# Last 64 GELU columns and the gate computed with tokens on partitions, in a gated mix of a state-space layer and a GELU feed-forward layer

## The chip, the cores and the metric

The kernel runs on one core of a Trainium2 chip. The metric is the time of one execution on the device, in microseconds (us). Beside it each run has a *span*, from the first to the last instruction of the profile. For the kernel before, the time is always 1.7 to 1.9 us longer than the span; this difference matters later.

Engines: PE is the tensor engine's matmul side, PEld its weight loads, DVE the vector engine, ACT the scalar (activation) engine, POOL the general-purpose one, SP the engine that issues most DMAs. "Moving columns" are the columns that a matmul streams through the array; the other operand, the weights, is loaded before. A *bank* is the piece of accumulation memory that a matmul writes.

## The reference, cut to what matters

There are 2,048 tokens of 640 values. A sigmoid gate per token mixes a state-space layer (`a`) with a feed-forward layer (`b`), whose hidden width is 1,728.

```
x = A_x                                             # [1, 2048, 640]
g = sigmoid((x * gate_w).sum(-1, keepdims=True))    # one number per token
a = state_space(x)                                  # input product, scan over tokens, output product, + x * Dskip
h = gelu(x @ w1 + b1)                               # [2048, 1728]
b = h @ w2 + b2
out = g * a + (1 - g) * b
```

1,728 is 13 x 128 + 64. The 14th tile of hidden columns has only 64 of them, and the kernel puts the gate's product beside it as a 65th column. This tile is what the change is about.

## The kernel before

Tokens go through in 4 chunks of 512. The first layer ("ff1") keeps the hidden columns on partitions: the weights of the matmul are a piece of `w1`, and the 512 tokens of the chunk move. The last tile thus streams all 512 columns for only 65 output partitions:

```
sizes = [P] * (KF - 1) + [F_LAST + 1]            # 13 tiles of 128, one of 65

def ff1_mm(p, c, kf, kd, t0=0, t1=CH):
    m = sizes[kf]
    w = ...                                       # m columns of w1, for the last tile 64 and gate_w
    nc.tensor.matmul(p[:m, t0:t1], lhsT=w, rhs=xT[c][:, kd, t0:t1], start=(kd == 0), stop=(kd == KD - 1))

def ff1_act(p, c, kf):
    m = min(sizes[kf], F - kf * P)
    nc.scalar.activation(out=gel[c][:m, kf, :], in_=p[:m, :], func=ACT.Gelu_apprx_tanh, bias=b1_c[:m, kf:kf + 1])
    if kf == KF - 1:
        # the gate: one partition, 512 tokens, then four DMAs that put it on the token partitions
        nc.scalar.activation(out=zrow[F_LAST:F_LAST + 1, :], in_=p[F_LAST:F_LAST + 1, :], func=ACT.Tanh, scale=0.5)
        for a in range(TPC):
            ti = c * TPC + a
            nc.sync.dma_start(out=gz[:, ti:ti + 1], in_=zrow[F_LAST:F_LAST + 1, a * P:(a + 1) * P])
```

The start loads its weights in pieces on the SP queue; `w1b` holds the hidden columns from 768 on:

```
for kd in range(KD):
    nc.sync.dma_start(out=w1b[kd][:, 0:F - cut1], in_=B_w1[kd * P:(kd + 1) * P, cut1:F])
# ... small parameters on the ACT queue, among them two loads of b1: 13 rows of 128, one row of 64 ...
nc.sync.dma_start_transpose(out=BT_re[:], in_=A_B_re[:, :])
nc.sync.dma_start_transpose(out=BT_im[:], in_=A_B_im[:, :])
```

The order on PE is: ff1 of chunk 0, then the state-space input product ("ssm") of chunk 0, ff1 and ssm of chunk 1, then for each chunk the second layer (`fin_b`) and the state-space output product (`fin_a`), with ssm and ff1 of the later chunks between.

Of the kernel before, what the change touches and what calls it, by code (L numbers as in the profile page):

```python
# [11 lines left out]
ACT = mybir.ActivationFunctionType  # L12
BF16 = mybir.dt.bfloat16
F32 = mybir.dt.float32
I32 = mybir.dt.int32

P = 128
T = 2048
D = 640
F = 1728  # L20
CH = 512
NCH = T // CH
KD = D // P
KS = D // P
KF = (F + P - 1) // P
F_LAST = F - (KF - 1) * P
NT = T // P
TPC = CH // P
HD = D // 2
FA = 6  # L30
# [8 lines left out]
def kernel(  # L39
# [19 lines left out]
    nc = tc.nc  # L59
# [4 lines left out]
    const = ctx.enter_context(tc.tile_pool(name="const", bufs=1))  # L64
# [7 lines left out]
    def bank(dtype=F32):  # L72
        return ps.tile([P, CH * 4 // (4 if dtype == F32 else 2)], dtype, name="bank")
# [3 lines left out]
    n1b = F - cut1 + 1  # L77
    xT = [const.tile([P, KD, CH], BF16, name=f"xT{c}") for c in range(NCH)]
    w1a = [const.tile([P, cut1], BF16, name=f"w1a_{kd}") for kd in range(KD)]
    w1b = [const.tile([P, n1b], BF16, name=f"w1b_{kd}") for kd in range(KD)]  # L80
# [6 lines left out]
    TSIN = const.tile([P, KS, CH], BF16, name="TSIN")  # L87
    ident = const.tile([P, P], BF16, name="ident")
    prmA = const.tile([3 * KS, P], BF16, name="prmA")
    NB = KS + KF  # L90
    prmB = const.tile([NB, P], BF16, name="prmB")
    colA = const.tile([P, 3 * KS], F32, name="colA")
    colB = const.tile([P, NB], F32, name="colB")
    Dbc = const.tile([P, D], BF16, name="Dbc")
    glast = const.tile([P, 2, KS], F32, name="glast")
    carry = const.tile([P, 2, KS], F32, name="carry")
    zrow = const.tile([P, CH], F32, name="zrow")
    gz = const.tile([P, NT], F32, name="gz")
    gcol = const.tile([P, 2, NT], F32, name="gcol")
    warm = work.tile([P, CH], BF16, name="v")  # L100
# [5 lines left out]
    lre_c = colA[:, 2 * KS:3 * KS]  # L106
    b1_c = colB[:, KS:NB]

# [15 lines left out]
    nc.sync.dma_start_transpose(out=xT[0][:, :, H * P:CH], in_=x2d[H * P:CH, :])  # L124
    for kd in range(KD):
        nc.sync.dma_start(out=w1b[kd][:, 0:F - cut1], in_=B_w1[kd * P:(kd + 1) * P, cut1:F])
    nc.gpsimd.memset(prmB[:], 0.0)
    make_identity(nc, ident[:])
    HC = CH // 4
    tfi = work.tile([P, HC], I32, name="e")  # L130
    nc.gpsimd.iota(tfi[:], pattern=[[1, HC]], base=0, channel_multiplier=0)
    nc.scalar.dma_start(out=prmB[KS:NB - 1, :], in_=B_b1[0:(KF - 1) * P].rearrange("(j p) -> j p", p=P))
    nc.scalar.dma_start(out=prmB[NB - 1:NB, 0:F_LAST], in_=B_b1[(KF - 1) * P:F].rearrange("(j p) -> j p", p=F_LAST))
    nc.scalar.dma_start(out=prmB[0:KS, :], in_=gate_w.rearrange("(j p) -> j p", p=P))
    nc.sync.dma_start_transpose(out=BT_re[:], in_=A_B_re[:, :])
    nc.sync.dma_start_transpose(out=BT_im[:], in_=A_B_im[:, :])
    nc.sync.dma_start_transpose(out=xT[1][:], in_=x2d[CH:2 * CH, :])
# [14 lines left out]
    class Clock:  # L152
        pe = 5.0
        act = 13.0
        dve = 0.0

    ck = Clock()
# [5 lines left out]
    def let_out(until):  # L163
        while pend:
            ready, cost, fn = pend[0]
            start = max(ck.dve, ready)
            if start >= until:
                return
            pend.pop(0)
            fn()  # L170
            ck.dve = start + cost
# [6 lines left out]
    def pe(cols):  # L178
        ck.pe += cols / 2400.0 + 0.002

    def act(cost):
        ck.act = max(ck.act, ck.pe + 0.2) + cost
        return ck.act
# [75 lines left out]
    hs = [None] * NCH  # L259
    gel = [None] * NCH  # L260
    gbs = [None] * NT
    sizes = [P] * (KF - 1) + [F_LAST + 1]

    def ff1_mm(p, c, kf, kd, t0=0, t1=CH):
        m = sizes[kf]
        w = w1a[kd][:, kf * P:kf * P + m] if kf < FA else w1b[kd][:, (kf - FA) * P:(kf - FA) * P + m]
        nc.tensor.matmul(p[:m, t0:t1], lhsT=w, rhs=xT[c][:, kd, t0:t1], start=(kd == 0), stop=(kd == KD - 1))  # L267
        pe(t1 - t0)

    def ff1_act(p, c, kf):  # L270
        m = min(sizes[kf], F - kf * P)
        nc.scalar.activation(out=gel[c][:m, kf, :], in_=p[:m, :], func=ACT.Gelu_apprx_tanh, bias=b1_c[:m, kf:kf + 1])  # L272
        act(0.69)
        if kf == KF - 1:
            nc.scalar.activation(out=zrow[F_LAST:F_LAST + 1, :], in_=p[F_LAST:F_LAST + 1, :], func=ACT.Tanh, scale=0.5)
            act(0.6)
            for a in range(TPC):
                ti = c * TPC + a
                nc.sync.dma_start(out=gz[:, ti:ti + 1], in_=zrow[F_LAST:F_LAST + 1, a * P:(a + 1) * P])

    def ff1(c, k0=0):
        for kf in range(k0, KF):
            p = bank()
            for kd in range(KD):
                ff1_mm(p, c, kf, kd)
            ff1_act(p, c, kf)
            let_out(ck.pe)

    def gel_tile(c):
        gel[c] = gelp.tile([P, KF, CH], BF16, name="gel")  # L290
        nc.gpsimd.memset(gel[c][F_LAST:F_LAST + 1, KF - 1, :], 1.0)


    gel_tile(0)
    banks = [bank() for _ in range(FA)]
    for kd in range(KD):
        for kf in range(FA):
            ff1_mm(banks[kf], 0, kf, kd, 0, HT)
# [10 lines left out]
    for kd in range(KD):  # L309
        for kf in range(FA):  # L310
            ff1_mm(banks[kf], 0, kf, kd, HT, CH)
        if kd == 2:
            nc.tensor.transpose(pA[:, P:P + NB], prmB[:], ident[0:NB, 0:NB])  # L313
            nc.vector.tensor_copy(out=colB[:], in_=pA[:, P:P + NB])
            for j in range(KD):
                nc.vector.tensor_copy(out=w1b[j][:, n1b - 1:n1b], in_=pA[:, P + j:P + j + 1])
    for kf in range(FA):
        ff1_act(banks[kf], 0, kf)
    ff1(0, FA)

    lo, hi = slice(0, HC), slice(HC, HB)
# [8 lines left out]
    for ks in range(KS):  # L330
        nc.vector.tensor_copy(out=TCOS[:, ks, 0:HB], in_=FC[:, ks, :])
        nc.vector.tensor_copy(out=TSIN[:, ks, 0:HB], in_=FS[:, ks, :])
        for dst, X, xs, Y in ((TCOS, FS, nsH, FC), (TSIN, FC, sH, FS)):
            t = work.tile([P, HB], F32, name="g")
# [194 lines left out]

    ssm(0)  # L530
    gel_tile(1)
    ff1(1)
    gates(0)
    ssm(1)
# [5 lines left out]
    load_xn(2)  # L540
    ssm(2)
    gel_tile(2)
    ff1(2)
    fin_b(1)
    gates(2)
# [41 lines left out]
```

## Time and profile before

The time before was 219.42 us, the median of 3 runs (219.11 to 219.45).

| what | value | view |
|---|---|---|
| span of the profiled run | 217.0 us | page, first line |
| PE busy | 212.2 us, 98% | page, part 1 |
| chain that ended last | 94% PE | page, part 4 |
| ff1 of a later chunk (14 tiles) | 15.11 us | windows |
| the last tile's 5 matmuls | 1.08 us | timeline |

First, lines of the page of the kernel before: span and number of instructions; busy time and share of each engine, with the number of its instructions; the DMA queue that fetches program code (packets, MB, share); and the chain of waits by engine.

```profile
span 217.0 us, 3363 instructions
...
PE 212.2 (98%) x1297; PEld 127.8 (59%) x1308; DVE 189.3 (87%) x393; ACT 94.1 (43%) x153; POOL 3.2 (1%) x12
...
q8 instruction: 10, 0.16, 0.3%
...
PE 94%; DMA 3%; issue 0%; SPq 0%; DVE 0%
```

PE sets the pace, with nothing but the first loads ahead of it. DVE waits once for the gate's DMA (`gz<-zrow`), for 1.9 us. The timeline of PE in the kernel before, around the last tile of chunk 0. Columns: start, duration, engine, line, what is written and read, weights (rows * columns), moving (rows x columns), count.

```profile
19.82 0.38 PE L267 MATMUL bank<-xT_76,w1b_85 128*65 128x512 bf16 x1
20.04 0.38 PE L267 MATMUL bank<-xT_76,w1b_86 128*65 128x512 bf16 x1
...
20.68 0.38 PE L267 MATMUL bank<-xT_76,w1b_89 128*65 128x512 bf16 x1
20.90 1.24 PE L448 MATMUL bank<-xT_76,BT_re 128*128 128x512 bf16 x5
```

Durations of matmuls overlap, so the *starts* are what counts: 216 ns apart, whether the weights have 65 columns or 128. And at the end of the same timeline, products of 128 columns:

```profile
213.32 0.44 PE L514 MATMUL bank<-CT_re,hs 128*128 128x128 bf16 x5
213.60 0.44 PE L514 MATMUL bank<-CT_im,hs 128*128 128x128 bf16 x5
```

Ten such matmuls, each with a full weight load of its own, start 56 ns apart (0.28 us for five). So weight loads hide at that pace. The Trainium skill ("TensorE: Matmul & The Clock Gate", section "Wait — 56ns, not 53.3ns?") gives moving columns / 2.4 GHz plus about 2.5 ns; these 56 and 216 ns agree.

The ff1 stretches of chunks 1, 2 and 3, in windows: from:to, length, then busy time and instructions of PE, PEld, DVE, ACT and POOL, the granted clock, DMA share, GB/s.

```profile
31.69:46.80 15.11, 15.01 (x69) 6.93 (x70) 14.63 (x40) 9.53 (x14) 0.00 (x0) 1.00 1.08 281
94.50:109.61 15.11, 15.01 (x70) 6.93 (x71) 14.81 (x27) 9.54 (x14) 0.00 (x0) 1.00 0.00 1
146.51:161.62 15.11, 15.01 (x69) 6.93 (x70) 14.83 (x28) 9.54 (x14) 0.00 (x0) 1.00 0.00 0
```

Two of its waits (who waited for what: us in total, times, longest), which the argument needs later:

```profile
DVE gcol L463 <- DMA gz<-zrow: 1.9, 1, 1.9
...
PEld L267 <- DMA w1b_89<-in_B_w_dram: 0.2, 1, 0.2
```

The second is small and easy to pass over. It says that in chunk 0 PE reaches `w1b` just as its last load lands: there is no slack there.

### The profile page before, as it was taken

What the parts mean: (1) busy time and instruction counts of PE and PEld (TensorE: products, weight loads), DVE (VectorE), ACT (ScalarE), POOL (GpSimd) and SP (SyncE); (2) the same over time, 40 slices, a digit from 0 to 9 for tenths busy, and PEclk for the clock granted to TensorE, in tenths of its full rate; (3) what the DMA queues carried; (4) which work ended last, traced back from release to release, by engine and by line L of the source; (5) the groups of instructions that cost most, each with busy time, mean ns of one, the idle gap of its engine ahead of it and who ended that gap; (6) DMA issues with size and microseconds to landing.
All of it is one profiled execution on the core that took longest, in us unless ns stands there. A gap on an engine that the chain in (4) does not pass through costs nothing.

```text
span 217.0 us, 3363 instructions
## 1 busy us (share of the span) xinstructions
PE 212.2 (98%) x1297; PEld 127.8 (59%) x1308; DVE 189.3 (87%) x393; ACT 94.1 (43%) x153; POOL 3.2 (1%) x12
## 2 busy tenths in 40 slices
PE   7999999999999999999999999999999999999994
PEld 4854444444577775444467777444457777777773
DVE  2899999969999999999999999999999999941153
ACT  2798656657696102556652200456663220022100
POOL 2001000000000000000000000000000000000000
PEclk9999999999999999999999999999999999999999
DMA  6999999970000025000000005100000000100011
GB/s 179 267 258 209 216 253 333 204 206 2 0 3 0 0 53 181 12 0 0 3 0 0 0 3 181 60 5 0 0 0 0 3 0 30 63 32 0 3 62 60
DMA packets 32326, 15.64 MB, mean 72 GB/s; under 512 B 25077, under 2 KB 32310, under 8 KB 32310
## 3 DMA queue, kind: packets, MB, share of 16 engines
q1 hardware_dynamic: 32098, 15.38, 28.2%
q8 instruction: 10, 0.16, 0.3%
q10 hardware_dynamic: 212, 0.04, 0.1%
q14 instruction: 6, 0.05, 0.1%
HBM read 7.22 MB, written 2.62 MB: 45 GB/s over the span
## 4 chain that ended last, share of the span: by engine, by line
PE 94%; DMA 3%; issue 0%; SPq 0%; DVE 0%
PE bank L495 28%; PE bank L267 26%; PE bank L514 20%; PE bank L448 20%; DMA xT_76<-in_A_x_dram 2%; DMA w1a_80<-in_B_w_dram 1%; SPq L116 0%; SPq L123 0%; DVE ot L519 0%; PE bank L313 0%
## 5 line engine op out<-in xcount | busy, mean ns | idle before, releaser
L495 PE MATMUL bank<-w_sb,gel 128*128 128x320 bf16 x448 | 61.6, 299 | 0.0
L495 PEld LDWEIGHTS <-gel 128*128 128x128 bf16 x448 | 43.7, 98 | 17.7
L272 ACT ACTIVATE gel<-bank,colB 128x512 bf16<-128x512 f32 (+1 forms) x56 | 37.3, 693 | 17.5 <-PE bank L267 17.5
L451 ACT ACTIVATE bu<-bank 128x512 bf16<-128x512 f32 x40 | 23.7, 597 | 38.9 <-PE bank L448 38.4
L514 PEld LDWEIGHTS <-hs 128*128 128x128 bf16 x330 | 31.8, 98 | 11.9
L404 DVE TENSOR_TENSOR_SCAN g<-r_c,carry,v 128x512 bf16<-128x512 f32 x30 | 37.1, 1270 | 0.0
L498 ACT ACTIVATE gb<-bank,gcol 128x320 f32<-128x320 f32 x32 | 16.4, 528 | 46.1 <-PE bank L495 44.6
L514 PE MATMUL bank<-CT_im,hs 128*128 128x320 bf16 (+2 forms) x165 | 27.1, 295 | 0.0
L514 PE MATMUL bank<-CT_re,hs 128*128 128x320 bf16 (+2 forms) x165 | 27.1, 295 | 0.0
L519 DVE SCALAR_TENSOR_TENSOR ot<-bank,gcol,gb 128x320 bf16<-128x320 f32 (+2 forms) x33 | 17.3, 532 | 8.6 <-PE bank L514 8.4
L481 DVE TENSOR_TENSOR bank<-xn,Dbc 128x320 f32<-128x320 bf16 (+2 forms) x33 | 14.5, 482 | 6.9 <-ACT gb L498 6.9
L448 PEld LDWEIGHTS <-BT_im 128*128 128x128 bf16 x100 | 9.8, 98 | 11.8
L448 PEld LDWEIGHTS <-BT_re 128*128 128x128 bf16 x100 | 9.8, 98 | 11.5
L385 DVE TENSOR_TENSOR v<-wa,wb 128x512 bf16<-128x512 bf16 x40 | 15.2, 421 | 0.6
L385 DVE TENSOR_TENSOR wa<-TCOS,g 128x1024 bf16<-128x1024 bf16 x20 | 13.7, 685 | 0.1
L385 DVE TENSOR_TENSOR wb<-TSIN,g 128x1024 bf16<-128x1024 bf16 x20 | 13.7, 684 | 0.0
L385 DVE TENSOR_TENSOR wb<-TSIN,bu 128x1024 bf16<-128x1024 bf16 x20 | 13.7, 684 | 0.0
L385 DVE TENSOR_TENSOR wa<-TCOS,bu 128x1024 bf16<-128x1024 bf16 x20 | 13.7, 683 | 0.0
L404 DVE TENSOR_TENSOR_SCAN g<-r_c,v 128x512 bf16<-128x512 f32 x10 | 11.8, 1210 | 0.0
L385 DVE TENSOR_TENSOR hs<-wa,wb 128x512 bf16<-128x512 bf16 x20 | 8.5, 424 | 0.7
L385 DVE TENSOR_TENSOR hs<-wb,wa 128x512 bf16<-128x512 bf16 x20 | 8.4, 418 | 0.0
L448 PE MATMUL bank<-xT_76,BT_im 128*128 128x512 bf16 x25 | 6.2, 379 | 0.0
(153 smaller groups left out, 243.1 us busy)
## 6 DMA issues: line engine op xcount, KB each, us to landing
out_dram<-ot SPq DMA_DIRECT2D x15, 160.0 KB, 1.8
w_sb<-in_B_w_dram SPq DMA_DIRECT2D x1, 2080.0 KB
xn<-in_A_x_dram SPq DMA_DIRECT2D x3, 640.0 KB, 4.8
xn<-in_A_x_dram SPq DMA_DIRECT2D x2, 320.0 KB
gz<-zrow SPq DMA_DIRECT2D x16, 0.5 KB, 2.0
w1b_85<-in_B_w_dram SPq DMA_DIRECT2D x1, 240.0 KB
w1b_86<-in_B_w_dram SPq DMA_DIRECT2D x1, 240.0 KB, 3.7
w1b_87<-in_B_w_dram SPq DMA_DIRECT2D x1, 240.0 KB
```

Source lines behind the costliest of these rows:

```text
L267: nc.tensor.matmul(p[:m, t0:t1], lhsT=w, rhs=xT[c][:, kd, t0:t1], start=(kd == 0), stop=(kd == KD - 1))
L272: nc.scalar.activation(out=gel[c][:m, kf, :], in_=p[:m, :], func=ACT.Gelu_apprx_tanh, bias=b1_c[:m, kf:kf + 1])
L385: nc.vector.tensor_tensor(out=o, in0=a, in1=b, op=op)
L404: nc.vector.tensor_tensor_scan(s["g"][:, ri, :], r_c[:, ks:ks + 1].to_broadcast([P, CH]), s["v"][:, ri, :], init, ALU.mult, ALU.add)
L448: nc.tensor.matmul(p[:], lhsT=BT[:, kd, ks * P:(ks + 1) * P], rhs=xT[c][:, kd, :], start=(kd == 0), stop=(kd == KD - 1))
L451: nc.scalar.activation(out=bu[:, ri, :], in_=p[:], func=ACT.Identity)
L481: dve_now(ck.pe, 0.45, lambda: nc.vector.tensor_tensor(out=p[:, 0:d1 - d0], in0=xn[c][:, a, d0:d1], in1=Dbc[:, d0:d1], op=ALU.mult))
L495: nc.tensor.matmul(p[:, 0:d1 - d0], lhsT=gel[c][:m, kf, lo:lo + P], rhs=w2_sb[:m, kf, d0:d1], start=(kf == 0), stop=(kf == KF - 1))
L498: nc.scalar.activation(out=gb[:, d0:d1], in_=p[:, 0:d1 - d0], func=ACT.Identity, scale=gcol[:, 1, ti:ti + 1])
L514: nc.tensor.matmul(p[:, 0:d1 - d0], lhsT=hs[c][:, j, lo:lo + P], rhs=CT[:, j % KS, d0:d1], start=False, stop=(j == 2 * KS - 1), skip_group ...
L519: nc.vector.scalar_tensor_tensor(out=ot[:, d0:d1], in0=p[:, 0:d1 - d0], scalar=gcol[:, 0, ti:ti + 1], in1=gbs[ti][:, d0:d1], op0=ALU.mult, ...
```

## The change

The intent: for the last tile let the 65 columns of `w1` move, and make the tokens the weights. A chunk then takes 4 token tiles x 5 input tiles = 20 matmuls of 65 moving columns, 1,300 columns in the place of 2,560. The gate comes out with tokens on partitions, where it is wanted, so its DMAs go. The bias now runs along the free dimension, while the activation call used so far takes one bias for each partition (`b1_c[:m, kf:kf + 1]`); so it is put into the bank first (the bank is "seeded"), by PE in chunk 0 and by ACT in the others. A DMA transpose turns the 64 GELU columns back for the second layer.

```
-    nc.scalar.dma_start(out=prmB[NB - 1:NB, 0:F_LAST], in_=B_b1[(KF - 1) * P:F]...)        # one row of b1
+    nc.sync.dma_start(out=b1x[:, 0:F_LAST], in_=B_b1[F - F_LAST:F]....to_broadcast([P, F_LAST]))   # after w1b, before BT_re
...
+    def last_bank(c):
+        p = bank()
+        pv = p[:, 0:TPC * NL].rearrange("p (a n) -> p a n", a=TPC)
+        if c == 0:
+            for a in range(TPC):
+                nc.tensor.matmul(pv[:, a, :], lhsT=ident[:], rhs=b1x[:], start=(a == 0), stop=True, skip_group_check=True)
+            return p, pv
+        nc.scalar.activation(out=pv, in_=b1x[:]....to_broadcast([P, TPC, NL]), func=ACT.Identity)
+        return p, pv
+
+    def last_tile(c, p, pv):
+        for a in range(TPC):
+            for kd in range(KD):
+                nc.tensor.matmul(p[:, a * NL:(a + 1) * NL], lhsT=xT[c][:, kd, a * P:(a + 1) * P],
+                                 rhs=w1b[kd][:, n1b - NL:n1b], start=False, stop=(kd == KD - 1), skip_group_check=True)
+        nc.scalar.activation(out=gelN[c % 2][:, :, 0:F_LAST], in_=pv[:, :, 0:F_LAST], func=ACT.Gelu_apprx_tanh)
+        nc.scalar.activation(out=gz[:, c * TPC:(c + 1) * TPC], in_=..., func=ACT.Tanh, scale=0.5)
+        nc.sync.dma_start_transpose(out=gel[c][:, KF - 1, :]..., in_=gelN[c % 2][:]...)

     def ff1(c, k0=0):
-        for kf in range(k0, KF):
+        for kf in range(k0, KF - 1):
             p = bank()
+            if kf == KF - 3:
+                last = last_bank(c)
             ...
+        last_tile(c, *last)
```

More of the change, by code (lines that the diff above doesn't have):

```diff
@@ L89 @@
     prmA = const.tile([3 * KS, P], BF16, name="prmA")
-    NB = KS + KF
+    NB = KS + KF - 1
     prmB = const.tile([NB, P], BF16, name="prmB")
@@ L96 @@
     carry = const.tile([P, 2, KS], F32, name="carry")
-    zrow = const.tile([P, CH], F32, name="zrow")
+    b1x = const.tile([P, F_LAST + 1], BF16, name="b1x")
+    gelN = [const.tile([P, TPC, P], BF16, name=f"gelN{i}") for i in range(2)]
     gz = const.tile([P, NT], F32, name="gz")
@@ L126 @@
         nc.sync.dma_start(out=w1b[kd][:, 0:F - cut1], in_=B_w1[kd * P:(kd + 1) * P, cut1:F])
-    nc.gpsimd.memset(prmB[:], 0.0)
     make_identity(nc, ident[:])
@@ L131 @@
     nc.gpsimd.iota(tfi[:], pattern=[[1, HC]], base=0, channel_multiplier=0)
-    nc.scalar.dma_start(out=prmB[KS:NB - 1, :], in_=B_b1[0:(KF - 1) * P].rearrange("(j p) -> j p", p=P))
-    nc.scalar.dma_start(out=prmB[NB - 1:NB, 0:F_LAST], in_=B_b1[(KF - 1) * P:F].rearrange("(j p) -> j p", p=F_LAST))
+    nc.gpsimd.memset(b1x[:, F_LAST:F_LAST + 1], 0.0)
+    for i in range(2):
+        nc.gpsimd.memset(gelN[i][:, :, F_LAST:P], 0.0)
+        nc.gpsimd.memset(gelN[i][:, :, F_LAST:F_LAST + 1], 1.0)
+    nc.scalar.dma_start(out=prmB[KS:NB, :], in_=B_b1[0:(KF - 1) * P].rearrange("(j p) -> j p", p=P))
     nc.scalar.dma_start(out=prmB[0:KS, :], in_=gate_w.rearrange("(j p) -> j p", p=P))
+    nc.sync.dma_start(out=b1x[:, 0:F_LAST], in_=B_b1[F - F_LAST:F].rearrange("(o d) -> o d", o=1).to_broadcast([P, F_LAST]))
     nc.sync.dma_start_transpose(out=BT_re[:], in_=A_B_re[:, :])
@@ L261 @@
     gbs = [None] * NT
-    sizes = [P] * (KF - 1) + [F_LAST + 1]
     def ff1_mm(p, c, kf, kd, t0=0, t1=CH):
-        m = sizes[kf]
-        w = w1a[kd][:, kf * P:kf * P + m] if kf < FA else w1b[kd][:, (kf - FA) * P:(kf - FA) * P + m]
-        nc.tensor.matmul(p[:m, t0:t1], lhsT=w, rhs=xT[c][:, kd, t0:t1], start=(kd == 0), stop=(kd == KD - 1))
+        w = w1a[kd][:, kf * P:(kf + 1) * P] if kf < FA else w1b[kd][:, (kf - FA) * P:(kf - FA + 1) * P]
+        nc.tensor.matmul(p[:, t0:t1], lhsT=w, rhs=xT[c][:, kd, t0:t1], start=(kd == 0), stop=(kd == KD - 1))
@@ L268, in ff1_mm @@
         pe(t1 - t0)
     def ff1_act(p, c, kf):
-        m = min(sizes[kf], F - kf * P)
-        nc.scalar.activation(out=gel[c][:m, kf, :], in_=p[:m, :], func=ACT.Gelu_apprx_tanh, bias=b1_c[:m, kf:kf + 1])
+        nc.scalar.activation(out=gel[c][:, kf, :], in_=p[:, :], func=ACT.Gelu_apprx_tanh, bias=b1_c[:, kf:kf + 1])
         act(0.69)
-        if kf == KF - 1:
-            nc.scalar.activation(out=zrow[F_LAST:F_LAST + 1, :], in_=p[F_LAST:F_LAST + 1, :], func=ACT.Tanh, scale=0.5)
-            act(0.6)
-            for a in range(TPC):
-                ti = c * TPC + a
-                nc.sync.dma_start(out=gz[:, ti:ti + 1], in_=zrow[F_LAST:F_LAST + 1, a * P:(a + 1) * P])
+    NL = F_LAST + 1
@@ new lines, in last_bank @@
+    def last_bank(c):
+        p = bank()
+        pv = p[:, 0:TPC * NL].rearrange("p (a n) -> p a n", a=TPC)
+        if c == 0:
+            for a in range(TPC):
+                nc.tensor.matmul(pv[:, a, :], lhsT=ident[:], rhs=b1x[:], start=(a == 0), stop=True, skip_group_check=True)
+            return p, pv
+        nc.scalar.activation(out=pv, in_=b1x[:].rearrange("p (o n) -> p o n", o=1).to_broadcast([P, TPC, NL]), func=ACT.Identity)
+        act(0.4)
+        return p, pv
[4 more added lines that the diff above has]
+                                 rhs=w1b[kd][:, n1b - NL:n1b], start=False, stop=(kd == KD - 1), skip_group_check=True)
+                pe(76)
+        nc.scalar.activation(out=gelN[c % 2][:, :, 0:F_LAST], in_=pv[:, :, 0:F_LAST], func=ACT.Gelu_apprx_tanh)
+        act(0.45)
+        nc.scalar.activation(out=gz[:, c * TPC:(c + 1) * TPC], in_=pv[:, :, F_LAST:NL].rearrange("p a o -> p (a o)"), func=ACT.Tanh, scale=0.5)
+        act(0.2)
+        nc.sync.dma_start_transpose(out=gel[c][:, KF - 1, :].rearrange("p (a t) -> p a t", a=TPC),
+                                    in_=gelN[c % 2][:].rearrange("p a n -> p (a n)"))
@@ L287, in ff1 @@
             let_out(ck.pe)
+        last_tile(c, *last)
+        let_out(ck.pe)
     def gel_tile(c):
         gel[c] = gelp.tile([P, KF, CH], BF16, name="gel")
-        nc.gpsimd.memset(gel[c][F_LAST:F_LAST + 1, KF - 1, :], 1.0)
     gel_tile(0)
```

## The prediction

> **What bounds the kernel now.** The tensor engine alone. The page gives it 212.2 us of a 217.0 us span (98%), clock granted 0.999. A busy PE is no proof by itself, but the chain of waits agrees: 94% of it is matmuls and nearly all the rest (3%) is the first DMAs. No wait of PE on another engine is longer than 1.2 us, and that one is the start. In the timeline matmuls start at even steps that follow the moving columns: 215.8 ns for 512, 136 ns for 320, 82 ns for 192, 55.9 ns for 128, which is columns / 2.4 GHz plus about 2.5 ns. The Trainium skill ("TensorE: Matmul & The Clock Gate", Wait — 56ns, not 53.3ns?) states this formula, and the trace agrees. So time is moving columns.
>
> **What the change removes.** The 14th GELU tile holds only 64 columns and the gate, so 5 matmuls of 512 moving columns per chunk fill 65 of 128 output partitions: 5 x 215.8 = 1,079 ns on PE per chunk, 4.3 us in all. Also one ACT tanh on one partition (590 ns) per chunk, 16 small gate DMAs (2.0 us to landing each), and one DVE wait of 1.9 us for them (at about 47 us).
>
> **What it adds.** 20 matmuls of 65 moving columns per chunk, each with its own 128x128 weight load; in chunk 0 four more for the bias; in chunks 1 to 3 one ACT seeding of 128x260, estimated 0.45 us from 0.53 us for 128x320. One DMA transpose per chunk, and a bias broadcast DMA at the start. The 65-row contraction in the second matmul stays.
>
> **The cost that decides.** By the formula a 65-column matmul is 65/2.4 + 2.5 = 29.6 ns. The question is whether the weight load hides. In the trace it does at 55.9 ns per pair (128 columns), and once two weight loads stand 15 ns apart (after the 15- to 19-column transposes, L313). Loads of 128 columns take 98 ns, of 65 columns 112 ns, so a full load occupies the array for less than its latency. The same page (Back-to-back issue gap) gives 81 ns for a pair at 128 columns; this trace shows 55.9, so I do not use it. I estimate 32 ns per pair: 20 x 32 = 640 ns against 1,079, 0.44 us saved per chunk, 1.76 us in four; less 4 x 32 = 0.13 us for the seeds of chunk 0: **1.6 us**. If pairs cannot go below 55.9 ns, the chunk costs 1,118 ns and the change loses 0.4 us.
>
> **Critical path.** All PE time counts. The rest should hide: ACT has about 0.36 us idle per GELU tile, and the seed is needed two tiles (2.2 us) after it can start. The transposed tile is first read 10.8 us after the first-layer matmuls of its chunk at the least (chunk 0: at about 59.5 us, issue at about 43.6). DVE is full until 190 us, but loses its 1.9 us wait, about what PE gains. The nearest hazard is BT_im, landing near 20.6 us, read at 21.8: the broadcast ahead of it costs about 0.5 us and PE comes 0.3 us earlier, which leaves about 0.4 us.
>
> **Predicted: 217.8 us, 217.2 to 218.8 in 8 of 10.** Faster by over 2%: 0.01; within 2%: 0.97; slower: 0.02.
>
> **What would show it.** Right: starts of the 65-column matmuls 30 to 35 ns apart in the timeline; PE still without waits; first-layer stretch of chunks 1 to 3 shorter by about 0.44 us; the DVE wait on the gate DMA gone. Wrong: starts at 50 ns or more; PE waiting at BT_im, at the seed, or at the transposed tile; DVE lateness turning into PE waits for banks.

## The result, and the profile after

The changed kernel took 218.87 us, the median of 6 runs (218.09 to 219.39), against 219.38 us (219.11 to 219.64) for the kernel before. The ratio is 0.9974, with a 95% interval of 0.9954 to 0.9993: 0.6 us faster by the means where 1.6 were predicted, and just outside the range given. (Ratios here are the mean time of one kernel's fast runs over that of the other's of the same rounds, so not quite the ratio of the medians quoted. For after_row and before_pad_j4 the recorded ratio fits the means only without the slow profiled run; with it they would be 0.9983 and 1.0012.) In a second measurement, after_copy below, the same kernel had a ratio of 0.9946.

The page of the changed kernel:

```profile
span 216.4 us, 3467 instructions
...
PE 210.8 (97%) x1361; PEld 128.0 (59%) x1372; DVE 189.3 (87%) x393; ACT 91.8 (42%) x156; POOL 1.6 (1%) x12
...
PE 92%; DMA 4%; SPq 2%; issue 0%; DVE 0%
```

The timeline of PE around the last tile of chunk 0:

```profile
20.57 0.59 PE L268 MATMUL bank<-xT,w1b 128*128 128x512 bf16 x2
21.00 0.78 PE L293 MATMUL bank<-w1b,xT 128*128 128x65 bf16 x20
21.62 1.24 PE L473 MATMUL bank<-xT,BT_re 128*128 128x512 bf16 x4
```

Twenty matmuls take 0.62 us; read one by one they start 30.7 ns apart on average. That is the mechanism of the prediction, even a little better (32 ns was the estimate). The ff1 windows of chunks 1 to 3 confirm it:

```profile
32.41:47.05 14.64, 14.54 (x85) 6.94 (x85) 14.23 (x41) 9.54 (x15) 0.00 (x0) 1.00 1.08 263
94.75:109.39 14.64, 14.54 (x85) 6.98 (x86) 14.39 (x25) 9.54 (x15) 0.00 (x0) 1.00 0.00 1
146.29:160.93 14.64, 14.54 (x84) 6.98 (x85) 14.36 (x28) 9.54 (x15) 0.00 (x0) 1.00 0.00 0
```

15.11 has become 14.64: 0.47 us in each chunk. Nothing waits for the transposes, and the DVE wait on the gate DMA is gone. So the saving is there. Cut into three at two marks, the first ssm matmul and the first matmul of the last `fin_a`, the two profiles show where it went (starts read from the trace, us):

| stretch | before | after | difference |
|---|---|---|---|
| start to the first ssm matmul (holds ff1 of chunk 0) | 20.90 | 21.62 | +0.72 |
| from there to the first matmul of the last `fin_a` | 182.08 | 180.68 | -1.40 |
| from there to the end of the span | 13.99 | 14.10 | +0.11 |

The middle gained 3 x 0.47. The start, which should have become 0.34 us shorter (0.47 less 0.12 for the four bias matmuls), became 0.72 longer. The waits of PE in the changed kernel say on what:

```profile
PEld L268 <- DMA w1b<-in_B_w_dram: 1.2, 2, 0.6
...
PE bank L268 <- DMA xT<-in_A_x_dram: 0.4, 1, 0.4
...
PE bank L268 <- DMA w1b<-in_B_w_dram: 0.3, 1, 0.3
```

Read matmul by matmul, the changed kernel lost 0.57 us at 9.1 us, where PE waited for the second half of `xT`, and 0.73 us at 13.5 and 14.2 us before `w1b` matmuls; the kernel before lost 0.23 us at 8.8 us and nothing later. The broadcast was issued only at 9.1 us, so the first of these stops is not its doing.

And there was a second oddity. The time exceeds the span by 1.79 to 2.99 us in the six runs, where the kernel before has 1.7 to 1.9. Something outside the first and last instruction had become longer too.

### The profile page after: what moved, and what is told of

It is laid out like the page before. It is cut to its first block, busy times and chain, and to the rows that moved or that the text cites. A ratio compares the mean times of both kernels' runs of the same rounds, so it can differ in the third digit from the quotient of the medians.

```text
span 216.4 us, 3467 instructions
## 1 busy us (share of the span) xinstructions
PE 210.8 (97%) x1361; PEld 128.0 (59%) x1372; DVE 189.3 (87%) x393; ACT 91.8 (42%) x156; POOL 1.6 (1%) x12
## 3 DMA queue, kind: packets, MB, share of 16 engines
q1 hardware_dynamic: 32114, 15.91, 30.1%
## 4 chain that ended last, share of the span: by engine, by line
PE 92%; DMA 4%; SPq 2%; issue 0%; DVE 0%
PE bank L520 28%; PE bank L268 22%; PE bank L539 20%; PE bank L473 20%; DMA w1b<-in_B_w_dram 3%; DMA xn<-in_A_x_dram 1%; PE bank L293 1%; SPq L127 1%; SPq L125 1%; SPq L124 0%; DVE ot L544 0%; PE bank L284 0%
## 5 line engine op out<-in xcount | busy, mean ns | idle before, releaser
L272 ACT ACTIVATE gel<-bank,colB 128x512 bf16<-128x512 f32 x52 | 34.8, 692 | 15.7 <-PE bank L268 14.7
L268 PE MATMUL bank<-xT,w1b 128*128 128x512 bf16 x136 | 31.0, 379 | 0.6 <-DMA w1b<-in_B_w_dram 0.3
L268 PE MATMUL bank<-xT,w1a 128*128 128x512 bf16 (+1 forms) x147 | 26.9, 336 | 0.6 <-DMA xT<-in_A_x_dram 0.4
L473 PE MATMUL bank<-xT,BT_im 128*128 128x512 bf16 x99 | 24.8, 379 | 0.1
L473 PE MATMUL bank<-xT,BT_re 128*128 128x512 bf16 x97 | 24.7, 379 | 0.2
L268 PEld LDWEIGHTS <-w1b 128*128 128x128 bf16 x140 | 13.5, 98 | 16.9 <-DMA w1b<-in_B_w_dram 1.2
L268 PEld LDWEIGHTS <-w1a 128*128 128x128 bf16 x150 | 14.4, 98 | 12.0 <-issue 0.6
L506 DVE TENSOR_TENSOR bank<-xn,Dbc 128x320 f32<-128x320 bf16 (+2 forms) x33 | 14.3, 483 | 5.7 <-ACT gb L523 5.7
```

What stands on the lines that cost most here:

```text
L268: nc.tensor.matmul(p[:, t0:t1], lhsT=w, rhs=xT[c][:, kd, t0:t1], start=(kd == 0), stop=(kd == KD - 1))
L272: nc.scalar.activation(out=gel[c][:, kf, :], in_=p[:, :], func=ACT.Gelu_apprx_tanh, bias=b1_c[:, kf:kf + 1])
L473: nc.tensor.matmul(p[:], lhsT=BT[:, kd, ks * P:(ks + 1) * P], rhs=xT[c][:, kd, :], start=(kd == 0), stop=(kd == KD - 1))
L506: dve_now(ck.pe, 0.45, lambda: nc.vector.tensor_tensor(out=p[:, 0:d1 - d0], in0=xn[c][:, a, d0:d1], in1=Dbc[:, d0:d1], op=ALU.mult))
```

## The experiments

Theories for the start. **A**: the bias broadcast (128 packets of 128 bytes, queued behind `w1b`) delays the tail of `w1b`. **B**: the first loads scatter from run to run, and one pair of profiles misleads. **C**: with one load fewer on the ACT queue, later DMA issues wait for other landings, and `w1b` comes late. For the end: the tensor engine's program is longer and its **code fetch** falls into the last microseconds; or the **transposes** or another part of the change do it.

Means of the spans, and the number of runs in which the time exceeded the span by more than 2.0 us, are given with each run. In five later comparisons (on four chips) the kernel before ran 55 times; its mean span was 217.6 to 217.9 and its time never exceeded the span by more than 1.86 us. One of the 55 had a span of 220.1 us, for a reason not known; it is in the comparison of before_pad, after_pad, after_row1_pad and before_less and makes their intervals wide.

### Both kernels again

No edit.

> The kernel before, unchanged, to see its scatter. Theory A (the change itself slows the start: the bias broadcast of 128 packets behind the last w1b load) and theory C (one DMA less on the ACT queue shifts which landing each later DMA issue waits for): spans near 217.0 us in every run, first matmul of the first layer to first matmul of the state-space input in chunk 0 near 15.6 us. Theory B (the start-up loads scatter from run to run, and the one profile of the changed kernel caught a bad one): spans scatter by 1 us or more and that stretch differs between profiles by 0.5 us or more.

> The changed kernel, unchanged. A and C: chunk 0 stretch again 16.3 to 16.5 us (before: 15.6), last w1b landing again near 14 us, spans 216.3 to 216.9. B: the stretch comes out near 15.3 us in this profile, and some spans lie near 215.3 us.

Measured: before_copy 219.39 us, ratio 1.0000 (0.9986 to 1.0015), spans 217.2 to 218.1, mean 217.65. after_copy 217.98 us, ratio 0.9946 (0.9925 to 0.9967), spans 215.9 to 216.6, mean 216.23, 2 of 6 runs with over 2.0 us outside the span. The first ssm matmul came at 21.52 us in before_copy (20.90 in the first profile of the same kernel) and at 21.18 us in after_copy (21.62).

So B holds in part: the start of an unchanged kernel moves by 0.6 us between profiles. In this pair the start is 0.34 us *shorter*, the number predicted; but that is partly luck. In before_copy the tensor clock was granted in full only 7.0 us after the first instruction, in after_copy after 6.2, and the 256-column matmuls up to there started 213 ns apart in the place of 109; in the first pair it was granted before the first ff1 matmul (5.1 and 5.0 us). before_copy lost 0.84 us to the slow clock and none to stops, after_copy 0.43 to the clock and 0.42 to a stop before `w1b`: by chance the same sum. With clock and stops taken off, the start is 0.34 to 0.35 us shorter in both pairs. What the change does to PE in chunk 0 is thus as predicted, and the +0.72 of the first pair is 1.07 us more of stops. The middle was again 1.40 us shorter. From here on, conclusions on the start rest on the means of spans of several runs, not on a pair of profiles.

### The broadcast alone, in the kernel before

```
+    nc.sync.dma_start(out=b1x[:, 0:F_LAST], in_=B_b1[F - F_LAST:F]....to_broadcast([P, F_LAST]))   # read by nobody
     nc.sync.dma_start_transpose(out=BT_re[:], in_=A_B_re[:, :])
```

> The kernel before plus the bias broadcast DMA alone, at the place that the change gave it, read by nobody. A: last w1b lands about 1 us later than in the kernel before (14 against 13.0 us), chunk 0 stretch about 16.3 to 16.7 us, span about 217.7 to 218. B and C: no change, stretch near 15.6, span near 217.0.

> before_b1x once more, on another chip: it had only 4 runs, spans 217.9, 218.1, 218.9 and 219.1 where before has 217.2 to 218.2. If the broadcast of 128 packets behind w1b costs time: spans again up to 219, mean 0.4 us or more over before. If that was chance: ratio 1.000 within 0.0015.

Measured: before_b1x 220.32 us, ratio 1.0040 (1.0019 to 1.0062), mean span 218.50. The repetition on another chip, before_b1x_2: 220.50 us, ratio 1.0049 (1.0027 to 1.0070), mean span 218.70, where before had 217.67. A small load that nobody reads costs 0.9 to 1.1 us of time. This is theory A, and a control separates the packets from the mere issue:

```
+    nc.sync.dma_start(out=b1x[0:1, 0:F_LAST], in_=B_b1[F - F_LAST:F]...)     # one row in the same place
```

> The kernel before plus one unread load of one 128 byte row at the place where the broadcast stood in before_b1x. If it was the 128 packets: ratio 1.000 (within 0.001). If it was the additional DMA issue on the SP queue itself (about 0.48 us before the BT transposes): 1.004 again, as before_b1x.

Measured: 219.47 us, ratio 1.0001 (0.9988 to 1.0015). So one more issue in this place costs nothing; the broadcast does. Windows of the start, of before_row and then of before_b1x_2, show it (columns as above; the last is GB/s). The profiled run of before_b1x_2 was the slowest of its six (span 219.5), so it shows the effect larger than the mean:

```profile
11.00:12.50 1.50, 1.50 (x15) 1.16 (x14) 0.81 (x7) 0.78 (x2) 0.00 (x0) 1.00 1.05 329
12.50:14.00 1.50, 1.45 (x11) 0.87 (x10) 1.47 (x3) 1.49 (x3) 0.00 (x0) 1.00 1.16 208
14.00:15.50 1.50, 1.50 (x9) 0.68 (x7) 1.47 (x3) 1.50 (x3) 0.00 (x0) 1.00 1.27 290
```

```profile
11.00:12.50 1.50, 1.50 (x15) 1.16 (x13) 0.89 (x7) 0.95 (x3) 0.00 (x0) 1.00 0.94 326
12.50:14.00 1.50, 1.43 (x9) 0.59 (x6) 1.47 (x3) 1.49 (x3) 0.00 (x0) 1.00 0.63 144
14.00:15.50 1.50, 0.00 (x0) 0.00 (x0) 1.47 (x3) 1.50 (x4) 0.00 (x0) 1.00 0.93 67
```

While the broadcast is under way the DMA engines move 144 and then 67 GB/s in the place of 208 and 290, and PE stands still. Its waits in before_b1x_2:

```profile
PEld L269 <- DMA w1b<-in_B_w_dram: 2.3, 2, 1.9
PE bank L269 <- DMA w1b<-in_B_w_dram: 1.6, 1, 1.6
```

The 128 packets themselves took 1.5 us of DMA engine time in sum, some 12 ns each, but they were spread from 12.4 to 15.3 us. The Trainium skill ("DMA: Bandwidth & Descriptors", section "Specifications") says that transfers under 512 bytes do not run at line rate; that the loads *beside* them slow down is not there. In the same stretch single 256-byte packets of the transposed load of `BT_re`, queued behind the broadcast, took up to 1.7 us (0.9 in before_row), so the two together may be what holds up the queue; why is not settled here.

### The broadcast moved, and taken out, in the changed kernel

after_b1x_act issues the same broadcast early on the ACT queue. after_noseed leaves the bias of the last 64 columns out altogether, with its broadcast, its matmuls and its ACT seeding (wrong, though within the tolerance).

```
-    nc.sync.dma_start(out=b1x[:, 0:F_LAST], ...)
+    nc.scalar.dma_start(out=b1x[:, 0:F_LAST], ...)        # after_b1x_act, after the load of gate_w
```
```
-        if c == 0: ... matmul of b1x ...                   # after_noseed: no seeding in any chunk
-        nc.scalar.activation(out=pv, in_=b1x[:]...)
-    ... start=False ...
+    ... start=(a == 0 and kd == 0) ...
```

> The changed kernel with the bias broadcast issued early on the ACT queue, in the place of the small load that was removed, so that the order of waits on the SP queue is that of before again. A: the tail of w1b is free again, chunk 0 stretch 15.2 to 15.6 us, span about 215.4 to 215.9; unless the early broadcast slows w1a instead. C: the same gain, so this run does not tell A from C; before_b1x does. B: no change beyond scatter.

> The changed kernel with the bias of the last 64 columns left out (a wrong result on purpose): no broadcast DMA, no seeding by the tensor engine or ACT. This is the change's core alone. If the 20 matmuls of 65 columns save 4 x 0.465 us and the broadcast is the only thing that gives some back: time 1.8 to 1.9 us under before (ratio about 0.9915), span about 215.8 where before has 217.7, no w1b wait of PE over 0.3 us. If the start-up loss has another cause (order of waits, chance): ratio stays near 0.994 to 0.995.

Measured: after_b1x_act 218.22 us, ratio 0.9941 (0.9926 to 0.9957), mean span 216.28. after_noseed 218.01 us, ratio 0.9938 (0.9921 to 0.9954), mean span 216.22. Both are misses for theory A as it was put: without any broadcast the changed kernel is no faster than after_copy (mean span 216.23). Its profile has two stops of 0.34 and 0.41 us before `w1b` matmuls, with no broadcast to cause them. In after_b1x_act these stops are gone, but it lost 0.54 us waiting for the second half of `xT`, as the first profile of the changed kernel did (0.57). So in the changed kernel the broadcast is at most a part of the loss.

### One load fewer on the ACT queue

```
-    nc.scalar.dma_start(out=prmB[NB - 1:NB, 0:F_LAST], in_=B_b1[(KF - 1) * P:F]...)
```

> The kernel before without the small load of the last bias row on the ACT queue (the last 64 biases become 0, a slightly wrong result on purpose); this is what after_noseed has left of the change at the start. Theory C (one load fewer on ACT shifts which landing each later issue waits for, and w1b lands late): time 0.3 to 0.5 us over before, PE waits over 0.3 us for w1b in the profile. Rival: ratio 1.000 within 0.001, no such wait.

Measured: 219.29 us, ratio 0.9983 (0.9947 to 1.0020), mean span 217.52. Theory C falls; its profile still has one stop of 0.29 us before `w1b`.

### One row and matmuls in the place of the broadcast

```
-    nc.sync.dma_start(out=b1x[:, 0:F_LAST], ....to_broadcast([P, F_LAST]))
+    nc.scalar.dma_start(out=b1row[:, 0:F_LAST], in_=B_b1[F - F_LAST:F]...)        # one row of 128 bytes
...
-                nc.tensor.matmul(pv[:, a, :], lhsT=ident[:], rhs=b1x[:], start=(a == 0), ...)
+                nc.tensor.matmul(p[:, a * NL:(a + 1) * NL], lhsT=ones[:], rhs=b1row[:], start=(a == 0), ...)   # a in 0..4
...
+        if c == 0:                                       # the fifth copy, for the ACT seeding of later chunks
+            nc.scalar.activation(out=b1x[:], in_=p[:, TPC * NL:(TPC + 1) * NL], func=ACT.Identity)
```

> The changed kernel with the bias fetched as one row of 128 bytes (in the place of the small load that the change removed) and spread over the partitions by five one-row matmuls in chunk 0, one of them copied out by ACT for the later seeds. Correct result. If the 128 packets of the broadcast are the loss: ratio 0.9915 to 0.9925, span about 215.9, the chunk 0 stretch about 0.3 us under that of before. If any bias seeding costs this much: near 0.9945.

Measured: 218.96 us, ratio 0.9973 (0.9952 to 0.9995), mean span 216.87: no better. But its profile was the key to the end. The stops before `w1b` were gone, and the last `fin_a` began at 201.95 us, earlier than in any run so far but after_copy (201.87); yet the span was 218.3. From the start of the last `fin_a` to the end it took 16.38 us, where the kernel before and its variants so far take 13.92 to 14.05. Three of the other five runs had 2.5 to 2.7 us outside the span.

### The end: transposes or code fetch

after_plain makes the four transposes plain copies (wrong result):

```
-        nc.sync.dma_start_transpose(out=gel[c][:, KF - 1, :]..., in_=gelN[c % 2][:]...)
+        nc.sync.dma_start(out=gel[c][:, KF - 1, :], in_=gelN[c % 2][:]...)
```

> The changed kernel with the four DMA transposes turned into plain SBUF to SBUF copies of the same tiles (a wrong result on purpose). In 7 of 12 runs of the changed kernel the time exceeds the span by 2.0 to 3.0 us, in all 17 of before by 1.8. If the transposes make this: time minus span is 1.8 in all runs, time about 0.3 us lower at the same span. If they don't: the same scatter stays. Span: no change, 216.2, since nothing waits for the transposes.

Measured: 218.27 us, ratio 0.9944 (0.9928 to 0.9959), mean span 216.20; still 2 of 6 runs over 2.0 us. The transposes are not it.

The other candidate is in part 3 of the page. The queue of kind "instruction" moves the program. Its 16 KB packets, held against the number of PE instructions begun by then, come like this (kernel before, before_copy and after_row, read from the trace):

```
before       192  420  667  954 1171 1433 1680 1938 2204 2454           of 2615 PE instructions
before_copy  194  420  667  948 1171 1433 1682 1940 2196 2454           of 2615
after_row    192  432  663  922 1170 1431 1685 1962 2198 2452  2742     of 2745
```

One fetch per some 250 recorded instructions, about as the Trainium skill has it ("Runtime: NRT & Kernel Launch", section "Instruction fetch mechanics"): blocks of 16 KB are 256 instructions, fetched by DMA while the program runs, at a cost that the page calls "mostly hidden". By this step the eleventh falls due at about 2,710, and in the longer programs measured later it came there (after 2,709 to 2,720 in after_pad, after_pad2 and before_pad2). The kernel before ends at 2,615 and never reaches it. The changed kernel ends at 2,744, close to the edge. In after_row the packet was seen, after 2,742: 16,384 bytes at 213.98 us, for 1.63 us, just as the last output stores went out. The trace goes on after the last instruction, and there it is in the first profile of the changed kernel, too: at 218.64 us, 2.24 us after the end of the span, for 0.98 us. This is the run with 2.99 us outside the span, the longest of all. The profiles of after_copy, after_b1x_act and after_plain (1.75, 1.75 and 2.09 us outside) have no eleventh packet.

Test: cut some 320-column matmuls into two of 160 (same work and 2.5 ns more for each) to bring the kernel before to the critical count, or to move the changed kernel away from it.

```
-                    nc.tensor.matmul(p[:, 0:d1 - d0], lhsT=..., rhs=...[:, ..., d0:d1], ...)
+                    for e0, e1 in (((d0, d0 + HD // 2), (d0 + HD // 2, d1)) if <some tiles> else ((d0, d1),)):
+                        nc.tensor.matmul(p[:, e0 - d0:e1 - d0], lhsT=..., rhs=...[:, ..., e0:e1], ...)
```

> The kernel before with 66 of its 320-column matmuls cut into two of 160 columns (same work, 132 instructions more on the tensor engine, 2,750 rows where the changed kernel has 2,746). By the clean step of 2.5 ns per matmul this costs 0.17 us. Code-fetch theory (the tensor engine fetches its program in blocks of 16 KB, one per 256 instructions; the added instructions bring an eleventh fetch into the last microseconds, beside the last output stores): time minus span exceeds 1.9 us in some runs, the DMA of kind instruction shows a 16 KB packet after 213 us, mean time 0.4 to 0.8 us over before. Rival (the longer end is from the transposes or from other parts of the change): time minus span 1.8 in every run, time 0.17 us over before.

> The changed kernel with 56 matmuls of the chunk-2 second layer cut in two (112 instructions more, cost 0.14 us by the step), which moves the eleventh fetch about 7 us ahead of the end, to 206 to 209 us. Code-fetch theory: time minus span 1.8 us in every run, stretch from the last product's start to the end of the span 14.0 us as in before; mean time 0.2 us or more under that of the changed kernel (ratio about 0.993) in spite of the added cost. Rival: time minus span scatters as before, time 0.14 us over the changed kernel.

Measured: before_pad 219.77 us, ratio 1.0014 (0.9978 to 1.0050), 1 of 6 runs over 2.0 us (2.90). The eleventh packet is in its profile, but 0.31 us after the end of the span, in a run with only 1.78 us outside: there it cost nothing, and the mean cost expected, 0.4 to 0.8 us, did not come. after_pad 218.41 us, ratio 0.9940 (0.9901 to 0.9979), 0 of 6 over 2.0 us (at most 1.82); its mean span of 216.60 includes a run whose profile shows a stop of 1.23 us before `w1b`. The cut matmuls of the second layer gave wrong columns (probably because two accumulations were started in one bank; not tested), so these two kernels and after_row1_pad serve for times only; the later ones cut the seeded `fin_a` and are correct.

after_row1_pad joins the padding with the one-row bias, now spread by a single matmul of 325 columns:

> The correct version with all that looked like a loss put right: bias by one row of 128 bytes and one matmul of 325 columns in chunk 0, the ACT queue with six loads as in before, and the padding of after_pad. If the broadcast, the load order and the fetch are the losses: saved 4 x 0.465 less 0.14 (seed) less 0.14 (pad), ratio 0.9925 to 0.9935, span about 216.0 with time minus span 1.8; better than after_pad by some 0.2 us. If the start-up loss is something else: no better than after_pad.

Measured: 218.12 us, ratio 0.9932 (0.9896 to 0.9968), mean span 216.40, nothing over 1.82 us outside the span in 5 runs.

Then both with correct results, on one chip:

> The changed kernel with the padding done in 60 matmuls of the last product of chunk 2, whose banks are seeded, so that the result is correct (after_pad gave wrong columns); 120 instructions more, cost 0.15 us. Code fetch: time minus span 1.8 us in every run. Broadcast still in: spans 216.1 to 217.3, mean near 216.6 as in after_pad.

> after_pad2 with the bias brought in as one row of 128 bytes and one matmul, in the place of the broadcast; correct result. If the broadcast costs time in some runs: spans 216.3 to 216.6 as in after_row1_pad, mean 0.2 to 0.3 us under after_pad2 and no w1b wait over 0.3 us; ratio about 0.993. If not: equal to after_pad2 within 0.1 us, since the one-row seed has a cost of 0.02 to 0.1 us of its own.

Measured: after_pad2 218.24 us, ratio 0.9946 (0.9926 to 0.9966), mean span 216.48. after_best 218.31 us, ratio 0.9947 (0.9929 to 0.9964), mean span 216.48. Neither has a run over 1.81 us outside the span. The two are equal, so the broadcast's removal did not pay in sum. The profiles show why it need not: after_pad2 stops 0.78 us before `w1b` and after_best does not; but the one-row seeding takes 0.24 us on PE where four identity matmuls take 0.12, and the stretch from the last `fin_a` to the end is 14.26 us against 14.10. These two add up to 0.28 us, so the broadcast should be worth about that much here. This is argued from one profile of each, not shown.

Over all, the padded kernels have 0 of 23 runs over 2.0 us, and the unpadded ones with 2,746 or 2,748 PE instructions (the changed kernel twice, after_b1x_act, after_plain, after_row) 13 of 30; after_noseed, with 8 fewer, had 0 of 6. The cure is clear. The cause in isolation needed three more runs:

> The kernel before with 70 matmuls of the last product of chunk 2 cut in two (correct result, 140 instructions more, cost 0.18 us), so that the eleventh fetch of the tensor engine's program is due some 3 us before its end. Code fetch: time minus span over 1.9 us in 2 or more of 6 runs, or a span over 218.5, mean time 0.4 us or more over before. Rival: time minus span 1.8 in all runs, spans near 217.9.

> The kernel before with 64 matmuls of the last product of chunk 2 cut in two (correct result): 2,746 rows on the tensor engine, exactly as many as the changed kernel. Code-fetch theory (a fetch that falls due within the last 35 or so instructions lands in the end of the program): time minus span over 2.0 us in some 4 of 10 runs, as in the changed kernel (13 of 30), taken together with before_pad_j5. Rival (something else of the change lengthens the end, and padding cured it by another way): time minus span 1.8 in every run. Cost of the cuts 0.17 us either way.

> The same with one more matmul cut: 2,748 rows, exactly as many as after_row, of whose 6 runs 3 had a time minus span of 2.5 us and one a span of 218.3. Same expectations as before_pad_j4.

Measured: before_pad2, whose fetch came at 213.1 us, 2 us ahead of the end of PE, had none over 2.0 us in 6 runs (one 1.95), ratio 1.0018 (0.9999 to 1.0037): by its expectation a miss, since a fetch that early does no visible harm. before_pad_j4 had 3 of 7 (2.04 to 2.10 us), ratio 0.9997 (0.9980 to 1.0015). Its profiled run, 221.58 us with a span of 219.7, is no evidence for the fetch: it has no eleventh packet and a last stretch of 13.99 us, and lost its time at the start and in a stop of 1.35 us at 75.9 us. before_pad_j5 had 1 of 6 (2.49), ratio 1.0008 (0.9984 to 1.0033), and its profile caught the fetch in the act. The DMA queue of program code has one packet more than in the kernel before:

```profile
q8 instruction: 11, 0.18, 0.3%
```

and of what SP waited for at the end, before_pad_j5 shows (the kernel before has "SPq L582 <- DMA out_dram<-ot: 1.6, 1, 1.6"):

```profile
SPq L583 <- DMA out_dram<-ot: 3.5, 1, 3.5
```

In after_row it was:

```profile
SPq L612 <- DMA out_dram<-ot: 3.7, 2, 3.5
```

In before_pad_j5 the packet began at 215.44 us and took 1.45 us. The last output packets then ended 3.31 us after PE's last matmul, where the kernel before has 1.59, and the last stretch took 15.91 us against 14.0. The packets tell why: of the 128 of the last store on the SP queue, 120 had begun by 215.62 us, and the other 8, a sixteenth, began only at 216.87, as the fetch ended (216.88). In after_row it is the same: 120 by 214.20, the other 8 from 215.59, the fetch until 215.61. So one DMA engine's share of the last store stood behind the fetch. This is the old kernel, with nothing of the change but about its number of instructions (2,748; the changed kernel has 2,746). So a program fetch can land among the last stores and cost nearly 2 us. That it costs less, or nothing, in most runs, and that its mean is not resolved in these ratios, is as plain. Of the runs in which only the part outside the span grew, the fetch is seen there in one, the first profile of the changed kernel; after_plain's profile, with 2.09 us outside, has none. For the others it is the likely reading, not a seen one.

## Why the prediction was right or wrong

**What bounds the kernel: right.** PE stayed at 97% busy and 92% of the chain.

**The deciding cost: right.** A 65-column matmul with its own full weight load takes 30.7 ns, estimated at 32; the formula alone gave 29.6. Chunks 1 to 3 gained 0.47 us each (0.44 predicted), the seed of chunk 0 took 0.12 us (0.13 predicted), and PE between the two marks became 1.40 us shorter in both pairs of profiles. Together with chunk 0 this is 3 x 0.47 + 0.34 = 1.75 us, a little over the predicted 1.6.

**"All PE time counts. The rest should hide": this step failed.** It priced what was added to PE, ACT and DVE, and of the DMAs looked only at whether their data come in time. Its sign "PE still without waits" did not come: in the first profile PE lost 0.73 us before `w1b` and 0.57 us on `xT`, against 0.23 us in the kernel before. Two things that it took for free were not:

1. *The start.* The prediction saw the broadcast as 0.5 us ahead of `BT_im`, with 0.4 us of slack. The nearer neighbour is *behind which* it was queued: the last load of `w1b`, on which PE had already waited 0.2 us in the profile before. In the kernel before, the broadcast alone costs 0.9 to 1.1 us. In the changed kernel its share is smaller, some 0.3 us by argument, and after_noseed shows that about 0.5 us is missing from the span even without it: 217.63 less 4 x 0.47 would be 215.75, against 216.22 measured. In its profile some 0.3 us of that is a longer last stretch (14.33 us; see the next point). Slow clock and stops together cost the start 0.8 to 1.8 us (mean 1.3) in the profiles of the seven changed kernels without the one-row bias, and 0.2 to 1.9 us (mean 0.9) in the eight of the kernel before without the broadcast. The scatter is as large as the difference, so the remainder, and the stop on `xT`, stay open.
2. *The end.* The 128 more PE instructions bring an eleventh program fetch to the edge of the program's end, where in some runs it falls among the last stores or just after the last instruction. In the two measurements of the changed kernel the time exceeded the span by 2.10 us on average (12 runs), against 1.8: 0.3 us, which the padding takes away. Inside the span the last stretch is 14.1 to 14.3 us in most of the changed kernels, padded or not, against 13.9 to 14.05 in the unpadded old one; this 0.1 to 0.3 us is also not explained.

The sum for after_copy, by means against before on the same chip: 1.75 us gained on PE, 1.42 us in the span, 1.21 us in the time. For the first measurement it is 0.58 us in the time; of what is missing there, some 0.4 us lies outside the span (2.19 us on average against 1.78), the rest inside it.

**What would have shown it.** The prediction named "starts 30 to 35 ns apart", "shorter by 0.44 us" and "the DVE wait gone" as signs of being right, and all three came; the fourth, PE without waits, did not. Its list of what could go wrong had the reading of `BT_im`, the seed, the transposed tile and banks; none of these waits appeared. The waits that did were on `xT` and `w1b`, and on the output stores.

**The range.** It allowed 1.0 us of loss against the middle, and only 0.6 of gain. The loss in the first measurement was 1.07 us. The timed runs of the changed kernel spread over 1.3 us, those of before over 0.5; a range with room for only 1.0 us of loss was too narrow.

No version tried beats the changed kernel by a margin that these runs resolve. after_pad2 and after_best have the steadiest ends.

## What to carry to other kernels

If the short side of a ragged tile moves, each matmul costs close to columns / 2.4 GHz + 2.5 ns, here down to 65 columns with a full weight load for each (30.7 ns against 29.6). When a change saves less than 1% of the time, look at the two ends as well as at the middle: which load PE is already waiting for at the start, and what a new small DMA behind it does; and how many instructions the program gains, if its last stores are on the critical path. And compare spans of several runs: the start of one unchanged kernel moved by 0.6 us between two profiles, as much as the whole effect. If only one pair of profiles is at hand, take off what each lost to a late clock and to stops before comparing.

## What the Trainium skill lacked or had wrong

- "TensorE: Matmul & The Clock Gate", section "Back-to-back issue gap", gives about 81 ns for a pair of weight load and matmul at 128 columns. These traces show 55.9 ns at 128 columns and 30.7 at 65, each with its own 128-column weight load.
- "Runtime: NRT & Kernel Launch", section "Instruction fetch mechanics", calls the cost of a 16 KB block "mostly hidden". In the middle of the program that agrees: ten fetches, and PE's steps stay even. At the end it does not: a fetch of 1.45 us among the last stores held up 8 of 128 store packets and made the last stretch 15.91 us in the place of 14.0 (before_pad_j5).
- No page says that a small broadcast load (128 packets of 128 bytes) slows the large load queued before it: 0.9 to 1.1 us of the kernel's time, DMA rate 144 and 67 GB/s against 208 and 290 in the same windows (the slowest of six runs).
